# A soft mixture of experts on one core: the output product made transposed in float32 on four row groups

## The chip, the core and the metric

One core of a Trainium2 chip runs one program. The time is device microseconds for the whole program, here the median of three runs. The engines that matter are TensorE (PE, with its weight loads shown as PEld), VectorE (DVE), ScalarE (ACT), GpSimd (POOL) and SyncE (SP), whose queue issues every transfer.

## The reference

The input x is 8 sequences of 2496 tokens with 256 values each. The reference takes the real part of a two-dimensional Fourier transform of each sequence and feeds the 19968 tokens to a soft mixture of experts with 8 experts of 4 slots, 32 slots in all:

```python
X = np.fft.fft(np.fft.fft(x, axis=1), axis=2).real        # 8 x 2496 x 256, then 19968 x 256
logits = X @ phi                                            # 19968 x 32
d = softmax(logits, over the tokens);  slot_input = d.T @ X # 32 x 256
slot_out[e] = relu(slot_input[e] @ w1[e]) @ w2[e]           # 32 x 256
c = softmax(logits, over the 32 slots)                      # 19968 x 32
out = c @ slot_out                                          # 19968 x 256, float32
```

The change concerns the last line alone: 19968 tokens by 32 slots, times 32 slots by 256 values, 20.45 MB of float32.

## The kernel before, in words

The sequences are taken in four pairs, p = 0 to 3. The length 2496 is split as 64 times 39, and mirrored columns are folded, so that the 2496 tokens of a sequence become 64 values of an index a by 20 columns k in two mirror halves. Parts a, t, b and c (line 210 on) load x, fold it and make the logits; parts e, d and u turn the token weights back and gather the slot inputs; part m joins the four pairs; parts l (line 465) and v (line 484) are the two expert products. All of this is the first 136 us, and the change does not touch it. What follows is touched.

Part r (line 498) takes the expert sums out of PSUM (`sos`, lines 506 and 507), replicates the 32 slots to four groups of 32 partitions with one product (line 508), and splits the result into a rounded part `rh[0]` (lines 510 and 511, ACT) and a remainder `rh[1]` (line 513, DVE). Both are 128 by 512, block diagonal for two columns k, and zero elsewhere (a memset, line 502).

Part s (line 520), once for each pair, transposes the logits so that the 128 partitions are tokens (lines 527 and 532), and makes the softmax over slots: in two halves of 20 columns k, a maximum (541, DVE), a subtraction (542, POOL), an exponential (543, ACT), a sum and reciprocal (544 to 546, DVE) and a product (547, POOL). The result `c` has 128 tokens on the partitions and 20 times 32 values behind each.

Part q (line 549) splits each half of `c` into a rounded part (553, ACT) and a remainder (554, DVE), side by side, in the single-pass type float32r.

Part o (line 560) runs 20 times, five for each pair. It transposes four blocks of 128 by 128 on TensorE (567), copies them out of PSUM (568, ACT), and makes four products of 128 tokens by two columns k by 256 values (574), each as two accumulating matmuls, with `rh[0]` and with `rh[1]`. The token weights `lT` are the stationary operand, the expert sums move. Each product fills one PSUM bank of 512 values and is copied to an output tile `ot` by ACT and DVE in turn (578). A finished tile of 8 KB on each partition (1 MB) leaves through SP (585). The fifth tile of each pair leaves in two pieces, 768 KB and, for the column that is its own mirror, 128 KB from 64 partitions (583). The first tile of all leaves in three pieces.

The output tiles are a ring of six (`RING`). The products use the pools `bank` (2 banks) and `bank3` (3 banks), the transposes `bank1` (2 banks). `ORDER` (line 39) lists the parts in priority; a planner with a cost model of its own then sets the order on each engine's queue, and an engine runs its queue in that order.

Of the kernel before, what the change touches and what calls it, by code (L numbers as in the profile page):

```python
# [6 lines left out]
F32 = mybir.dt.float32  # L7
F32R = mybir.dt.float32r
AF = mybir.ActivationFunctionType
ALU = mybir.AluOpType  # L10
# [4 lines left out]
NA, NCF, NKC = 64, 39, 20  # L15
NPAIR = 4
D = 256
NSLOT = 32
# [17 lines left out]
FIRST = [0, 1]  # L36
P1, P2, P3, PM = 2, 2, 3, 0
W2 = [1, 1, 1, 1, 1, 1, 1, 1, 1, 1, 1, 2, 2, 1]
ORDER = (
# [6 lines left out]
).split()  # L46

# [66 lines left out]
    return out, where  # L114


def _build(nc, tc, xh, phih, w1h, w2h, cins, where, out, out0):
    from contextlib import ExitStack, nullcontext

    v, sc, pe = nc.vector, nc.scalar, nc.tensor  # L120
    ctx = ExitStack()
    with ctx:
        cp = ctx.enter_context(tc.tile_pool(name="cp", bufs=1))
        sb = ctx.enter_context(tc.tile_pool(name="sb", bufs=1))
# [4 lines left out]
        def ring(name):  # L129
            return sb.tile([128, 8, D], F32, name=name, tag="ring", bufs=RING)  # L130
# [19 lines left out]
        def bank1(name, dt=F32):  # L150
            return p1.tile([128, 512], dt, name=name, tag="p1")
# [33 lines left out]
        ps = bank("psphi")  # L185
# [14 lines left out]
        tok = cp.tile([128, NPAIR], F32, name="tok")  # L200
# [219 lines left out]
        anchor = {}  # L420
# [41 lines left out]
        rh = []  # L462
# [34 lines left out]

        def part_r():
            so = sos_[0]
            for j in range(2):  # L500
                rh.append(sb.tile([128, 2, D], F32R, name=f"rh{j}", tag="d", bufs=2))
                nc.gpsimd.memset(rh[j].bitcast(F32), 0.0)
            v.tensor_copy(identr, ident)
            sos = sb.tile([128, D], F32, name="sos", tag="dpm", bufs=2)
            ps = bank("sorep")
            sc.copy(sos[:, :128], so[:, :128])
            v.tensor_copy(sos[:, 128:], so[:, 128:D])
            pe.matmul(ps[:, :D], C("sel2"), sos, start=True, stop=True)
            half = [slice(0, 64), slice(64, 128)]
            sc.copy(rh[0][half[0], 0, :], ps[half[0], :D])  # L510
            (v.tensor_copy if RH else sc.copy)(rh[0][half[1], 1, :], ps[half[1], :D])
            for k, r in enumerate(half):
                v.tensor_tensor(rh[1][r, k, :], ps[r, :D], rh[0][r, k, :].bitcast(F32), op=ALU.subtract)

        identr = sb.tile([128, 128], F32R, name="identr", tag="mex2", bufs=1)


        hl, cq = {}, {}

        def part_s(p):  # L520
            L = lt[p]
            cq[p] = sb.tile([128, 40, NSLOT], F32, name=f"c{p}", tag=CT[p], bufs=bufs_(CT[p]))
            for b in range(3):
                ps = bank1(f"cT{p}_{b}")
                n = min(4, NG - 4 * b)
                for j in range(n):
                    pe.transpose(  # L527
                        ps[:, 120 * j : 120 * j + 120],
                        L[:, 4 * b + j].rearrange("p s k -> p (s k)"), ident[:120, :120],
                    )  # L530
# [5 lines left out]
            e1 = nc.gpsimd if GP & 1 else v  # L536
            e2 = nc.gpsimd if GP & 2 else v
            for i in range(2):
                c = cq[p][:, 20 * i : 20 * i + 20]
                m = sb.tile([128, 2, 20], F32, name=f"cm{p}_{i}", tag="cm", bufs=2)  # L540
                v.tensor_reduce(m[:, 0], c, axis=AX.X, op=ALU.max)  # L541
                e1.tensor_tensor(c, c, m[:, 0].unsqueeze(2).to_broadcast([128, 20, NSLOT]), op=ALU.subtract)  # L542
                sc.activation(c, c, AF.Exp)
# [3 lines left out]
                e2.tensor_tensor(c, c, m[:, 1].unsqueeze(2).to_broadcast([128, 20, NSLOT]), op=ALU.mult)  # L547

        def part_q(p, i):
            c = cq[p][:, 20 * i : 20 * i + 20]  # L550
            e3 = nc.gpsimd if GP & 4 else v
            t = sb.tile([128, 20, 2, NSLOT], F32R, name=f"hl{p}_{i}", tag=HT[i], bufs=bufs_(HT[i]))
            sc.copy(t[:, :, 0], c)
            e3.tensor_tensor(t[:, :, 1], c, t[:, :, 0].bitcast(F32), op=ALU.subtract)
            hl[p, i] = t


        n_ev = [0]

        def part_o(p, b):  # L560
            ps = bank1(f"lT{p}_{b}", F32R)
            lT = et([128, 4, 128], f"lTs{p}_{b}", F32R)
            with tc.issue_after(anchor["v1"]) if LA and p == 0 else nullcontext():
              for i in range(4):
                k0 = 8 * b + 2 * i
                src = hl[p, k0 // 20][:, k0 % 20 : k0 % 20 + 2].rearrange("p k h s -> p (k h s)")
                pe.transpose(ps[:, i * 128 : i * 128 + 128], src, identr)  # L567
            sc.copy(lT, ps.rearrange("p (i n) -> p i n", i=4))  # L568
            ot = ring(f"o{p}_{b}")
            done = 0  # L570
            for i in range(4):
                po = (bank, bank3)[i % 2](f"po{p}_{b}_{i}")
                for j in range(2):
                    pe.matmul(  # L574
                        po, lT[:, i, :], rh[j].rearrange("p k d -> p (k d)"), start=j == 0, stop=j == 1,
                    )
                np_ = 64 if b == 4 and i == 3 else 128
                (v.tensor_copy if n_ev[0] % 2 else sc.copy)(  # L578
                    ot[:np_, 2 * i : 2 * i + 2, :].rearrange("p k d -> p (k d)"), po[:np_]
                )  # L580
                n_ev[0] += 1
                if b == 4 and i == 3:
                    nc.sync.dma_start(out0[p].rearrange("p (r d) -> p r d", d=D), ot[:64, 6:8])
                elif i == 3 or (b == 4 and i == 2) or ((p, b) == (0, 0) and i in FIRST):
                    nc.sync.dma_start(
                        out[p, :, (8 * b + done) * D : (8 * b + 2 * i + 2) * D].rearrange("p (r d) -> p r d", d=D),
                        ot[:, done : 2 * i + 2],
                    )
                    done = 2 * i + 2

        def after(f, *a):
            at_ = {0: None, 1: anchor.get("u"), 2: anchor.get("l")}[CAFTER]
# [63 lines left out]
```

## Time and profile before

| | |
|---|---|
| median of three runs (lowest, highest) | 197.49 us (197.16, 197.59) |
| span of the profiled execution, first to last instruction | 195.7 us |
| launch and end around the span, taken as 197.49 less 195.7 | 1.8 us |
| PE, PEld, DVE, ACT, POOL busy, share of the span | 88%, 63%, 67%, 65%, 13% |
| HBM read, written | 38.46 MB, 20.45 MB |
| mean granted TensorE clock | 0.988 of full speed |

The page gives no time of its own for the profiled execution beside its span; where a sum is made against the span, the 1.8 us are added back. In the rows below a time in the first column is counted from the start of the span. `L574` is line 574 of the kernel before. A row of a group gives count, busy time in us, mean length of one in ns, and after the bar the idle time before them with what ended it. Matmuls on TensorE overlap, so that a mean length is longer than the distance between two of them. A float32 matmul shows as two records.

### The profile page before, as it was taken

To read this page: it belongs to the slowest core of one execution; us is meant where nothing else is said; L and a number is where in the kernel's file an instruction comes from. 1 tells how busy PE (TensorE), PEld (TensorE's weight loads), DVE (VectorE), ACT (ScalarE), POOL (GpSimd) and SP (SyncE) were. 2 spreads that over 40 slices of the span, in tenths; PEclk is the share of its full clock that TensorE was granted. 3 is DMA by queue.
4 is the path that set the end of the run, shared out by engine and by line. 5 is a ranking of instruction groups with operands and counts; after the bars stand their busy time and mean duration, and the time that the engine had idled before them with its cause. 6 is when DMAs were issued, how large, how long until landed. Compare 5 with 4: busy or idle time off the path is not lost.

```text
span 195.7 us, 4290 instructions
## 1 busy us (share of the span) xinstructions
PE 173.1 (88%) x1690; PEld 124.3 (63%) x1690; DVE 131.5 (67%) x238; ACT 127.4 (65%) x277; POOL 24.6 (13%) x27
## 2 busy tenths in 40 slices
PE   0499999979999999989999989999999999989900
PEld 0376685557768877567765857256788867768600
DVE  0599868999977973712457534895777888966600
ACT  2135675579767696676848756754877988997610
POOL 0000000000000000000000202577003257310000
PEclk9999999999999999999999999999999999999995
DMA  5999999999970899200770969970199999799996
GB/s 182 406 424 411 422 415 422 419 422 373 372 286 8 266 383 425 104 0 0 240 284 20 321 230 343 417 308 0 64 384 375 407 403 398 304 417 365 430 427 214
DMA packets 10707, 59.17 MB, mean 302 GB/s; under 512 B 1344, under 2 KB 1728, under 8 KB 5696
## 3 DMA queue, kind: packets, MB, share of 16 engines
q1 hardware_dynamic: 10688, 58.91, 76.7%
q8 instruction: 13, 0.21, 0.4%
q14 instruction: 6, 0.05, 0.1%
HBM read 38.46 MB, written 20.45 MB: 301 GB/s over the span
## 4 chain that ended last, share of the span: by engine, by line
PE 79%; ACT 8%; DVE 3%; DMA 2%; POOL 2%; issue 2%; SPq 0%; ACTq 0%; DVEq 0%; POOLq 0%
PE po L574 17%; PE pt L231 10%; PE z L238 8%; PE e L329 7%; PE a L273 6%; PE u L371 6%; PE d L346 4%; PE h L470 4%; PE so L490 4%; PE lp L291 3%; PE lm L292 3%; PE cT L527 3%; DMA x<-xh 2%; PE lT L567 2%; POOL c L542 2%; ACT et L232 2%
## 5 line engine op out<-in xcount | busy, mean ns | idle before, releaser
L574 PE MATMUL po<-rh,lTs 128*128 128x512 f32 x160 | 42.4, 405 | 1.6 <-ACT lTs L568 0.7
L231 PE MATMUL pt<-cs,eo 128*128 128x128 f32 x160 | 26.4, 297 | 8.7 <-DVE eo L226 7.6
L574 PEld LDWEIGHTS po<-rh,lTs 128*128 128x128 f32 x160 | 28.1, 188 | 8.6 <-ACT o L578 1.8
L578 DVE COPY o<-po 128x512 f32<-128x512 f32 (+1 forms) x40 | 26.9, 685 | 7.9 <-PE po L574 6.9
L232 ACT COPY et<-pt 128x512 f32<-128x512 f32 x40 | 23.0, 594 | 13.8 <-PE pt L231 13.2
L231 PEld LDWEIGHTS pt<-cs,eo 128*128 128x128 f32 x160 | 19.5, 151 | 15.5 <-DVE eo L226 7.6
L578 ACT COPY o<-po 128x512 f32<-128x512 f32 x40 | 23.2, 595 | 7.4 <-PE po L574 7.1
L224 DVE TENSOR_TENSOR x<-x 128x1024 f32<-128x1024 f32 x16 | 19.4, 1214 | 3.2 <-DMA x<-xh 3.2
L238 PE MATMUL z<-et,wphi 128*32 128x256 f32 (+1 forms) x288 | 19.0, 371 | 0.9 <-ACT et L232 0.8
L542 POOL TENSOR_TENSOR c<-c,cm 128x640 f32<-128x640 f32 x8 | 11.8, 1487 | 28.0 <-DVE cm L541 27.0
L314 ACT ACTIVATE d<-lt,nm 120x128 f32<-120x128 f32 x44 | 13.6, 392 | 2.1 <-DVE nm L311 2.0
L226 DVE TENSOR_TENSOR eo<-x 128x512 f32<-128x512 f32 x20 | 13.6, 681 | 0.6 <-PE u L371 0.3
L227 DVE TENSOR_TENSOR eo<-x 128x512 f32<-128x512 f32 x20 | 13.6, 678 | 0.0
L329 PE MATMUL e<-cs,dpm 120*64 120x120 f32 x176 | 13.5, 273 | 0.0
L238 PEld LDWEIGHTS z<-et,wphi 128*32 128x32 f32 x288 | 7.8, 113 | 8.3 <-ACT et L232 3.2
L329 PEld LDWEIGHTS e<-cs,dpm 120*64 120x64 f32 x176 | 10.7, 136 | 3.5 <-issue 2.0
L354 ACT COPY ds<-d 64x320 f32<-64x320 f32 x24 | 10.0, 420 | 4.1 <-PE d L346 3.4
L547 POOL TENSOR_TENSOR c<-c,cm 128x640 f32<-128x640 f32 x8 | 11.0, 1389 | 10.0 <-DVE cm L546 5.5
L568 ACT CAST lTs<-lT 128x512 fp32r<-128x512 f32 x20 | 11.5, 600 | 0.9 <-PE lT L567 0.9
L273 PE MATMUL a<-cs,zt 128*120 128x128 f32 x88 | 11.4, 279 | 0.6 <-ACT zt L264 0.6
L371 PE MATMUL u<-eo,ds 128*32 128x129 f32 x320 | 11.6, 275 | 0.0
L273 PEld LDWEIGHTS a<-cs,zt 128*120 128x120 f32 x88 | 10.2, 183 | 1.9 <-ACT zt L264 1.3
(99 smaller groups left out, 245.3 us busy)
## 6 DMA issues: line engine op xcount, KB each, us to landing
x<-xh SPq DMA_DIRECT2D x16, 1024.0 KB, 11.2
out<-o SPq DMA_DIRECT2D x15, 1024.0 KB, 5.8
w<-w1h SPq DMA_DIRECT2D x6, 1024.0 KB, 9.2
w<-w2h SPq DMA_DIRECT2D x12, 512.0 KB, 6.0
x<-xh SPq DMA_DIRECT2D x4, 896.0 KB, 11.0
out<-o SPq DMA_DIRECT2D x4, 768.0 KB, 6.1
w<-w1h SPq DMA_DIRECT2D x4, 512.0 KB, 6.3
w<-w2h SPq DMA_DIRECT2D x2, 1024.0 KB, 6.9
```

The source lines that it names most:

```text
L224: v.tensor_tensor(x[:, 0:4], x[:, 0:4], x[:, 4:8], op=ALU.add)
L226: v.tensor_tensor(e[:, :, 0:128], x[:, 0:4, 0:128], x[:, 0:4, 128:256], op=ALU.add)
L227: v.tensor_tensor(e[:, :, 128:256], x[:, 0:4, 0:128], x[:, 0:4, 128:256], op=ALU.subtract)
L231: pe.transpose(b[:, g * 128 : g * 128 + 128], e[:, g, k * 128 : k * 128 + 128], ident)
L232: sc.copy(tr[k][:, :, :, qi, :], b.rearrange("p (g h a) -> p g h a", g=4, h=2))
L238: pe.matmul(z[32 * g : 32 * g + 32, o : o + n], wphi[:, w, :], tr[k][:, g].rearrange("p h q a -> p (h q a)"), start=i != 1, stop=i != 0, t ...
L273: pe.matmul(ps[:120, i * 128 : i * 128 + 128], zt[p][:, GS * g : GS * g + GS].rearrange("p s h c -> p (s h c)"), C("wa"), start=True, stop ...
L329: pe.matmul(ps[64 * k : 64 * k + 64, 120 * i : 120 * i + 120], dpm[p, hf][:, k, 3 * j + i, :], C(name), start=True, stop=True, tile_positi ...
L371: last = pe.matmul(ub[32 * g : 32 * g + 32, 0:129], dsb[p][:, k, c, :], e[:, 0:129] if k == 0 else e[:, 127:256], start=cc == 0, stop=cc == 9,
L542: e1.tensor_tensor(c, c, m[:, 0].unsqueeze(2).to_broadcast([128, 20, NSLOT]), op=ALU.subtract)
L574: pe.matmul(po, lT[:, i, :], rh[j].rearrange("p k d -> p (k d)"), start=j == 0, stop=j == 1,)
L578: (v.tensor_copy if n_ev[0] % 2 else sc.copy)(ot[:np_, 2 * i : 2 * i + 2, :].rearrange("p k d -> p (k d)"), po[:np_])
```

## The change

The output product is turned round. The expert sums become the stationary operand and stay float32 (`rh[0]`, one tile of 128 by 256, four copies of the 32 slots), the token weights move, and the result has 128 of the 256 values on the partitions and tokens behind them. For this the 32 slots must lie on partitions: VectorE's block transpose turns each 32 by 32 block of `c`, so that partition group g holds the slots of the 32 tokens that were on it. The four groups are multiplied one by one, each with 32 rows of the array (`tile_position=(32 * g, 0)`), into four PSUM banks. The split into rounded part and remainder, TensorE's transposes and their copies, the zeroed block-diagonal tiles and the small 128 KB transfers go. The columns k are now cut 16 and 24 in place of 20 and 20 (`KP`); the tiles b = 0 to 3 take 16 columns and one half of the 256 values, the tile b = 4 the last eight columns and both halves. The products go round seven banks, those of `bank1` among them. In `ORDER`, `q01` and `q11` come earlier and `s20` moves ahead of `o10`. The host undoes the new layout.

```diff
+KP = ((0, 16), (16, 24))
-    "u30 m00 l00 s00 l10 q00 s10 v00 v10 r00 o00 q01 o01 q10 o02 o03 "
-    "o04 o10 s20 q11 o11 q20 o12 o13 q21 o14 s30 o20 o21 q30 o22 o23 "
+    "u30 m00 l00 s00 l10 q00 s10 v00 q01 v10 r00 o00 o01 q10 o02 q11 o03 "
+    "o04 s20 o10 o11 q20 o12 o13 q21 o14 s30 o20 o21 q30 o22 o23 "
...
         def part_r():
             so = sos_[0]
-            for j in range(2):
-                rh.append(sb.tile([128, 2, D], F32R, name=f"rh{j}", tag="d", bufs=2))
-                nc.gpsimd.memset(rh[j].bitcast(F32), 0.0)
-            v.tensor_copy(identr, ident)
+            rh.append(sb.tile([128, D], F32, name="rh", tag="mex2", bufs=1))
...
-            pe.matmul(ps[:, :D], C("sel2"), sos, start=True, stop=True)
-            half = [slice(0, 64), slice(64, 128)]
-            sc.copy(rh[0][half[0], 0, :], ps[half[0], :D])
-            (v.tensor_copy if RH else sc.copy)(rh[0][half[1], 1, :], ps[half[1], :D])
-            for k, r in enumerate(half):
-                v.tensor_tensor(rh[1][r, k, :], ps[r, :D], rh[0][r, k, :].bitcast(F32), op=ALU.subtract)
+            for k in range(2):
+                dk = slice(128 * k, 128 * k + 128)
+                pe.matmul(ps[:, dk], C("sel2"), sos[:, dk], start=True, stop=True)
+            v.tensor_copy(rh[0], ps[:, :D])
...
         def part_q(p, i):
-            sc.copy(t[:, :, 0], c)
-            e3.tensor_tensor(t[:, :, 1], c, t[:, :, 0].bitcast(F32), op=ALU.subtract)
+            r0, n = KP[i]
+            t = sb.tile([128, n, NSLOT], F32, name=f"ct{p}_{i}", tag=HT[i], bufs=bufs_(HT[i]))
+            v.transpose(t.rearrange("p k s -> p (k s)"), cq[p][:, r0 : r0 + n].rearrange("p k s -> p (k s)"))
...
+        BANKS = [bank, bank3, bank1, bank3, bank, bank1, bank3]
         def part_o(p, b):
-            ps = bank1(f"lT{p}_{b}", F32R)
-            lT = et([128, 4, 128], f"lTs{p}_{b}", F32R)
-                pe.transpose(ps[:, i * 128 : i * 128 + 128], src, identr)
-            sc.copy(lT, ps.rearrange("p (i n) -> p i n", i=4))
-            for i in range(4):
-                po = (bank, bank3)[i % 2](f"po{p}_{b}_{i}")
-                for j in range(2):
-                    pe.matmul(
-                        po, lT[:, i, :], rh[j].rearrange("p k d -> p (k d)"), start=j == 0, stop=j == 1,
-                    )
+            if b < 4:
+                t, r0, dcs = hl[p, b // 2], 0, [b % 2]
+            else:
+                t, r0, dcs = hl[p, 1], 16, [0, 1]
+            for g in range(4):
+                n = 16 if b < 4 else 8 if g < 2 else 6
+                w = n * NSLOT
+                po = BANKS[n_ev[0] % 7](f"po{p}_{b}_{g}")
+                rows = slice(32 * g, 32 * g + 32)
+                mv = t[rows, r0 : r0 + n].rearrange("p k s -> p (k s)")
+                for j, dc in enumerate(dcs):
+                    pe.matmul(
+                        po[:, j * w : j * w + w], rh[0][rows, 128 * dc : 128 * dc + 128], mv,
+                        start=True, stop=True, tile_position=(32 * g, 0),
+                    )
+                (v.tensor_copy if n_ev[0] % 2 else sc.copy)(ot[:, o : o + w * len(dcs)], po[:, : w * len(dcs)])
...
-                if b == 4 and i == 3:
-                    nc.sync.dma_start(out0[p].rearrange("p (r d) -> p r d", d=D), ot[:64, 6:8])
...
+                if g == 3 or (p, b) == (0, 0):
+                    nc.sync.dma_start(out[p, b, :, done:o], ot[:, done:o])
```

More of the change, by code (lines that the diff above doesn't have):

```diff
@@ L35 @@
 GP = 3
-FIRST = [0, 1]
 P1, P2, P3, PM = 2, 2, 3, 0
@@ L114, in _tables, with _build @@
     return out, where
-def _build(nc, tc, xh, phih, w1h, w2h, cins, where, out, out0):
+def _build(nc, tc, xh, phih, w1h, w2h, cins, where, out):
     from contextlib import ExitStack, nullcontext
@@ L507, in part_r @@
             v.tensor_copy(sos[:, 128:], so[:, 128:D])
-            pe.matmul(ps[:, :D], C("sel2"), sos, start=True, stop=True)
-            half = [slice(0, 64), slice(64, 128)]
-            sc.copy(rh[0][half[0], 0, :], ps[half[0], :D])
-            (v.tensor_copy if RH else sc.copy)(rh[0][half[1], 1, :], ps[half[1], :D])
-            for k, r in enumerate(half):
-                v.tensor_tensor(rh[1][r, k, :], ps[r, :D], rh[0][r, k, :].bitcast(F32), op=ALU.subtract)
-        identr = sb.tile([128, 128], F32R, name="identr", tag="mex2", bufs=1)
+            for k in range(2):
+                dk = slice(128 * k, 128 * k + 128)
+                pe.matmul(ps[:, dk], C("sel2"), sos[:, dk], start=True, stop=True)
+            v.tensor_copy(rh[0], ps[:, :D])
         hl, cq = {}, {}
@@ L535, in part_s @@
                 )
[L536 to L540, printed above, removed]
+            for i, (r0, n) in enumerate(KP):
+                c = cq[p][:, r0 : r0 + n]
+                m = sb.tile([128, 2, 24], F32, name=f"cm{p}_{i}", tag="cm", bufs=2)[:, :, :n]
                 v.tensor_reduce(m[:, 0], c, axis=AX.X, op=ALU.max)
-                e1.tensor_tensor(c, c, m[:, 0].unsqueeze(2).to_broadcast([128, 20, NSLOT]), op=ALU.subtract)
+                nc.gpsimd.tensor_tensor(c, c, m[:, 0].unsqueeze(2).to_broadcast([128, n, NSLOT]), op=ALU.subtract)
                 sc.activation(c, c, AF.Exp)
@@ L546, in part_s @@
                 v.reciprocal(m[:, 1], m[:, 1])
-                e2.tensor_tensor(c, c, m[:, 1].unsqueeze(2).to_broadcast([128, 20, NSLOT]), op=ALU.mult)
+                nc.gpsimd.tensor_tensor(c, c, m[:, 1].unsqueeze(2).to_broadcast([128, n, NSLOT]), op=ALU.mult)
         def part_q(p, i):
-            c = cq[p][:, 20 * i : 20 * i + 20]
-            e3 = nc.gpsimd if GP & 4 else v
-            t = sb.tile([128, 20, 2, NSLOT], F32R, name=f"hl{p}_{i}", tag=HT[i], bufs=bufs_(HT[i]))
-            sc.copy(t[:, :, 0], c)
@@ L562, in part_o @@
-            lT = et([128, 4, 128], f"lTs{p}_{b}", F32R)
-            with tc.issue_after(anchor["v1"]) if LA and p == 0 else nullcontext():
-              for i in range(4):
[L565 to L570, printed above, removed]
@@ L571, in part_o @@
-            for i in range(4):
-                po = (bank, bank3)[i % 2](f"po{p}_{b}_{i}")
-                for j in range(2):
+            ot = ring(f"o{p}_{b}").rearrange("p r d -> p (r d)")
+            if b < 4:
+                t, r0, dcs = hl[p, b // 2], 0, [b % 2]
+            else:
+                t, r0, dcs = hl[p, 1], 16, [0, 1]
+            done = o = 0
+            for g in range(4):
[5 more added lines that the diff above has]
+                for j, dc in enumerate(dcs):
@@ L574, in part_o @@
                     pe.matmul(
-                        po, lT[:, i, :], rh[j].rearrange("p k d -> p (k d)"), start=j == 0, stop=j == 1,
-                    )
-                np_ = 64 if b == 4 and i == 3 else 128
-                (v.tensor_copy if n_ev[0] % 2 else sc.copy)(
-                    ot[:np_, 2 * i : 2 * i + 2, :].rearrange("p k d -> p (k d)"), po[:np_]
-                )
+                        po[:, j * w : j * w + w], rh[0][rows, 128 * dc : 128 * dc + 128], mv,
+                        start=True, stop=True, tile_position=(32 * g, 0),
+                    )
@@ L581, in part_o @@
+                (v.tensor_copy if n_ev[0] % 2 else sc.copy)(ot[:, o : o + w * len(dcs)], po[:, : w * len(dcs)])
+                o += w * len(dcs)
                 n_ev[0] += 1
-                if b == 4 and i == 3:
[L583 to L589, printed above, removed]
+                if g == 3 or (p, b) == (0, 0):
+                    nc.sync.dma_start(out[p, b, :, done:o], ot[:, done:o])
+                    done = o
@@ L637 @@
     ]
-    out = nc.dram_tensor("out", (NPAIR, 128, 38 * D), F32, kind="ExternalOutput").ap()
-    out0 = nc.dram_tensor("out0", (NPAIR, 64, 2 * D), F32, kind="ExternalOutput").ap()
+    out = nc.dram_tensor("out", (NPAIR, 5, 128, 8 * D), F32, kind="ExternalOutput").ap()
     with tile.TileContext(nc, schedule_with_timeline_sim=True) as tc:
-        _build(nc, tc, *ins[:4], ins[4:], where, out, out0)
+        _build(nc, tc, *ins[:4], ins[4:], where, out)
     r = _run(nc, [arrays], core_ids=[0])
-    got = r.results[0]["out"].reshape(NPAIR, 2, NA, 19, 2, D)
-    got0 = r.results[0]["out0"].reshape(NPAIR, NA, 2, D)
+    got = r.results[0]["out"]
+    main = got[:, :4].reshape(NPAIR, 2, 2, 128, 2, 2, 8, 2, 32)
+    tok = np.empty((NPAIR, 2, 2, NKC, NA, D), np.float32)
+    tok[:, :, :, :16] = main.transpose(0, 7, 4, 1, 6, 5, 8, 2, 3).reshape(NPAIR, 2, 2, 16, NA, D)
+    o = 0
+    for g in range(4):
+        n = 4 if g < 2 else 3
+        last = got[:, 4, :, o : o + 2 * n * 64].reshape(NPAIR, 128, 2, n, 2, 32)
+        o += 2 * n * 64
+        tok[:, :, g // 2, 16 : 16 + n, 32 * (g % 2) : 32 * (g % 2) + 32] = last.transpose(0, 4, 3, 5, 2, 1).reshape(
+            NPAIR, 2, n, 32, D
+        )
     full = np.empty((NPAIR, 2, 2496, D), np.float32)
@@ L648 @@
     kc, ka = k % NCF, k % NA
-    for h in range(2):
-        for half, sel in ((0, (kc > 0) & (kc < NKC)), (1, kc >= NKC)):
-            row = kc[sel] - 1 if half == 0 else NCF - kc[sel] - 1
-            full[:, h, k[sel]] = got[:, half, ka[sel], row, h]
-        sel = kc == 0
-        full[:, h, k[sel]] = got0[:, ka[sel], h]
+    row = np.where(kc == 0, NKC - 1, np.where(kc < NKC, kc, NCF - kc) - 1)
+    full[:, :, k] = tok[:, :, (kc >= NKC).astype(int), row, ka]
     return full.reshape(8 * 2496, D)
```

## The prediction

> **What bounds the kernel now.** I read the page first, then the busy time by stretches, then the chain that ended last and the timelines of the engines around the first output.
>
> ```profile
> span 195.7 us, 4290 instructions
> ```
>
> ```profile
> 138.00:186.30 48.30, 46.71 (x246) 36.67 (x246) 37.83 (x63) 39.03 (x73) 11.15 (x8) 1.00 0.90 362
> 141.00:194.00 53.00, 43.89 (x233) 34.35 (x232) 35.02 (x59) 36.99 (x69) 11.15 (x8) 0.97 0.96 386
> 141.00:149.00 8.00, 8.00 (x45) 6.68 (x45) 5.57 (x9) 5.87 (x12) 0.00 (x0) 1.00 0.97 389
> 150.00:162.00 12.00, 11.59 (x69) 9.12 (x68) 10.36 (x20) 10.79 (x22) 4.99 (x4) 1.00 1.00 415
> 180.00:191.00 11.00, 6.12 (x28) 4.30 (x26) 4.25 (x7) 4.58 (x8) 0.00 (x0) 1.00 1.02 423
> 149.00:150.00 1.00, 1.00 (x6) 0.82 (x5) 0.70 (x1) 0.72 (x2) 0.00 (x0) 1.00 0.64 160
> 162.00:163.00 1.00, 1.00 (x8) 0.60 (x7) 1.00 (x3) 1.00 (x3) 0.70 (x1) 1.00 0.82 270
> 167.00:169.00 2.00, 1.88 (x11) 1.46 (x11) 2.00 (x6) 1.82 (x5) 0.00 (x0) 1.00 0.39 153
> 178.00:180.00 2.00, 2.00 (x13) 1.68 (x11) 1.28 (x3) 1.45 (x4) 0.00 (x0) 1.00 0.99 301
> 191.00:192.00 1.00, 0.00 (x0) 0.00 (x0) 0.00 (x0) 0.00 (x0) 0.00 (x0) 0.52 0.90 207
> ```
>
> These are stretches of the span: length, busy time of PE, PEld, DVE, ACT and POOL, then granted clock, busy share of the DMA engines and GB/s. The first row looks like a stage bound by TensorE: 46.71 of 48.30 us busy. But from 180 to 191 TensorE is busy for 6.12 us only: it ends near 186, while bytes move until 194 (386 GB/s for 53.0 us are the whole 20.45 MB). Almost 8 us of transfers are still to come when the last product is done. From 141 to 194 the DMA engines are 96% busy, and 20.45 MB leave at 386 GB/s. In undisturbed stretches the rate is 415 and 423, so 419 is the ceiling that I use, and 20.45 MB at 419 take 48.8 us. The stage is bound by the transfers, with 53.0 - 48.8 = 4.2 us of losses, which lie in a few places. A faster TensorE cannot by itself give more than those losses and an earlier first transfer.
>
> Two kinds of loss can be named. The first:
>
> ```profile
> L583 SPq DMA_DIRECT2D out<-o x4: 472/609/1220, 148.2 to 186.0; - x4
> ...
> DMA to landing us min/median/max: 3.1/4.9/6.9
> ```
>
> These are the four small transfers of 128 KB from 64 partitions. One is issued for each pair, 148.2 to 186.0, and lands some us later; after each there is one dip in GB/s with the engines still nearly busy. Against 419 the rows at 149, 162, 178 and 191 lose 0.62 + 0.36 + 0.56 + 0.51 = 2.05 us. The second is 167 to 169, with the DMA engines 39% busy: 2 x (1 - 153/419) = 1.27 us lost because nothing was queued. The chain of waits shows why:
>
> ```profile
> 161.42 0.75 DVE cm L541
> 162.30 3.68 POOL c L542 x2
> 166.01 0.20 ACT c L543
> ```
>
> The copies out of PSUM stand on the ACT and DVE queues behind the next pair's softmax, which waits for POOL. With TensorE needing about as long for a tile as the transfer of it, no stock of finished tiles covers that.
>
> **The change part by part.** The costs of the old output product:
>
> ```profile
> L574 PE MATMUL po<-rh,lTs 128*128 128x512 f32 x160 | 42.4, 405 | 1.6 <-ACT lTs L568 0.7 <-ACT o L578 0.6 <-ACT rh L511 0.2
> ...
> L574 PEld LDWEIGHTS po<-rh,lTs 128*128 128x128 f32 x160 | 28.1, 188 | 8.6 <-ACT o L578 1.8 <-ACT lTs L568 1.8 <-issue 0.3
> L578 DVE COPY o<-po 128x512 f32<-128x512 f32 (+1 forms) x40 | 26.9, 685 | 7.9 <-PE po L574 6.9
> ...
> L578 ACT COPY o<-po 128x512 f32<-128x512 f32 x40 | 23.2, 595 | 7.4 <-PE po L574 7.1
> ...
> L568 ACT CAST lTs<-lT 128x512 fp32r<-128x512 f32 x20 | 11.5, 600 | 0.9 <-PE lT L567 0.9
> ...
> L567 PE MATMUL lT<-identr,hl 128*128 128x128 f32 x80 | 9.0, 243 | 0.0
> ...
> L554 DVE TENSOR_TENSOR hl<-c,hl 128x640 fp32r<-128x640 f32 x8 | 7.1, 883 | 0.0
> ...
> L527 PE MATMUL cT<-cs,lt 120*128 120x120 f32 x44 | 6.1, 271 | 0.0
> ...
> L482 DVE STREAM_TRANSPOSE hT<-hs 128x512 f32<-128x512 f32 x4 | 2.7, 678 | 0.1
> ```
>
> *TensorE.* A tile of 1 MB now costs 42.4/20 = 2.12 us of products and 9.0/20 = 0.45 us of transposes, which overlap a little, against 1.049/0.419 = 2.50 us for its transfer. After the change a tile costs four float32 matmuls of 512 columns on 32 rows each. No row here shows row groups. The nearest is the first expert product, also float32, 512 columns and cut in four, but by output columns:
>
> ```profile
> L470 PE MATMUL h<-w,sT x64: 592/592/617, 121.7 to 129.6; 128*32 128x512 f32 x64
> ```
>
> ```profile
> 121.66 2.78 PE L470 MATMUL h<-w,sT 128*32 128x512 f32 x24
> ```
>
> The code has 32 such matmuls and the trace 64 records, so each is two records. 24 records took 2.78 us; with the last one's tail of about 0.17 (0.592 less the distance) taken off, a set of four records takes (2.78 - 0.17)/6 = 0.43 us. That four really run at once is seen from an undivided float32 product:
>
> ```profile
> 111.75 2.55 PE L346 MATMUL d<-e,cs 128*128 128x320 f32 x8
> ```
>
> There eight records of 320 columns take 2.55 us, about 0.3 us each with the tail, or 0.4 to 0.5 for 512 columns: one undivided record costs what the set of four does. So the new tile costs 2 x 0.43 = 0.86 us if the four row groups run at once, 1.72 if two do, and 8 x 0.43 = 3.44 if they take turns. Eight weight loads of 128 columns at 188 ns, if nothing hid them and they came singly, are 1.5 us. I take 0.9 to 1.7 us; anything below 2.50 gives the same end, since the transfers then set the pace. The Trainium skill (page "TensorE: Matmul & The Clock Gate", section "Part 3: Packing small matmuls") gives four row groups of 512 columns a measured speedup of 3.07; by that a tile would cost an estimated 3.44/3.07 = 1.1 us. No run here shows it yet, and the sum would be the same.
>
> *ACT and DVE.* The copies stay 80, taken in turn, four for a tile: 2 x 0.685 = 1.37 us of DVE and 2 x 0.595 = 1.19 us of ACT, each under 2.50. ACT loses the 20 casts of `lT` (11.5 us) and the rounding in part q. DVE loses the remainders (7.1 us) and gains block transposes: 512 elements cost 0.678, 768 in proportion 1.02, so 4 x 1.70 = 6.8 us. DVE is even, ACT lighter by over 11.5 us. POOL and the reductions handle the same number of elements, cut 16 and 24. All of it is beside the transfers and costs nothing while tiles are in stock; tiles will be in stock, since two engines empty a tile in 1.4 us where its transfer takes 2.5, and the ring holds six. That stock also covers a queue that waits for POOL: the 1.27 us go. What is late next is the ring itself: copies will wait for a transfer to free a tile, and behind them on ACT and DVE stands the next pair's softmax, with up to five tiles, 12 us, to cover it.
>
> *Transfers.* The bytes are the same: 4 x (4 x 128 x 2048 + 128 x 1792) x 4 = 20.45 MB. The four 64-partition transfers go, their bytes travel in full-width tiles of 7 KB rows: 2.05 us saved. The first tile leaves in four pieces rather than three. Of the slow start (141 to 149 at 389 GB/s, 8 x (1 - 389/419) = 0.57 us) I count half, 0.3, as saved.
>
> *First output.*
>
> ```profile
> 136.53 0.70 PE L508 MATMUL sorep<-sos,cs 128*128 128x256 f32 x2
> ...
> 137.29 0.38 ACT L510 CAST rh<-sorep 64x256 fp32r<-64x256 f32 x1
> ...
> 138.07 0.86 DVE L513 TENSOR_TENSOR rh<-sorep,rh 64x256 fp32r<-64x256 f32 x2 [1.60 <-ACT rh L511]
> ...
> 139.63 1.28 ACT L578 COPY o<-po 128x512 f32<-128x512 f32 x2 [0.22 <-PE po L574]
> ...
> 140.24 0.35 SPq L585 DMA_DIRECT2D out<-o  x1
> ```
>
> Now: two ACT casts, then two subtractions until 138.93, then products; the first copy starts at 139.63. After: the replicating product, in two halves with the same columns, ends about as before; one DVE copy of 256 elements, priced like one of the two subtractions at 0.43, from 137.29 to 137.72; then the first matmul, two records, 0.43 + 0.59 = 1.02 us with up to 0.19 of weight load; the copy starts at 138.8 to 139.0. The first transfer is 0.7 us earlier. Bounds: 1.2 earlier if the first half's early start counts, 1.0 later if the two transposes of the next part q (0.68 + 1.02) stand ahead of the copy on DVE.
>
> *Sum.* 2.05 + 1.27 + 0.3 + 0.7 = 4.3 us. 195.7 - 4.3 = 191.4 us of span, plus the 1.8 us around it (197.49 - 195.7): 193.2 us.
>
> **The rivals.**
>
> *The row groups take turns.* Against it: the column groups above run at once. For it: nothing in this trace shows rows divided. For each pair TensorE then needs 4 x 3.44 + 8 x 0.43 x 1792/2048 = 16.8 us, for four 67.1, plus half of the 6.1 us of softmax transposes (L527, two pairs of four): from 137.7 to 207.9, then a copy, 0.7, the last tile's transfer, 2.5, and the 1.7 from 194.0 to the end: span 212.8, time 215 us. It decides as soon as a tile costs over 2.50 us, that is with fewer than 1.4 groups at once. Chance 0.11.
>
> *The clock falls.* With TensorE idle since about 186 the row at 191 shows a clock of 0.52. If the lighter TensorE lost its clock during the stage, two groups at once would cost 2 x 1.72 = 3.44 us for a tile, again 215 us, but four at once 1.72 and no harm. Against it: pauses would be about 1.5 us, not 5. The Trainium skill (same page, "Part 1: The HAM clock gate") has the clock halve after an idle window of about 3.4 us; the row at 191 agrees. Chance 0.02.
>
> *Only the small transfers matter.* The queues stall as before and the first output is no earlier: 197.5 - 2.05 - 0.3 = 195.1 us. For it: the softmax chain over ACT, DVE and POOL is kept, and the planner orders it anew. Against it: the stock of tiles. Chance 0.10.
>
> *Nothing remains.* A planner's order that puts several softmax steps ahead of the first output delays it by about 4 us and eats the gain: 197.5, or a little over. Chance 0.05.
>
> **How the numbers follow.** My forecast has chance 0.72. Its own range is 191.6 (start 1.2 earlier, all 4.2 us of losses gone, 423 GB/s in place of 419) to 194.9 (start 1.0 later). The range for all is 191.5 to 196.8, reaching over the third rival with a start 1.7 late; it leaves out the first two, and most of the fourth. Faster by over 0.2% (0.4 us, about what a measurement of this kernel can tell from no change): 0.72 + 0.10 = 0.82; within that 0.03; slower 0.11 + 0.02 + 0.02 = 0.15.
>
> **What would show it.** Right: the records of a tile's four matmuls start together and a tile takes 0.9 to 1.7 us; the first output transfer is issued near 139.5; GB/s stays near 419 from there, with no dips in the stage; TensorE idles at the ring. Wrong: matmul records of different groups one behind another and TensorE busy to the end; clock below 1.00 in the stage; gaps in DMA share behind a softmax; the first issue after 140.24.

## The result and the profile after

The changed kernel takes 203.05 us (median of four runs, 202.1 to 203.3), beside 197.32 us for the kernel before on the same chip: ratio 1.0287 [1.026, 1.0314]. It is 5.7 us slower. The forecast was 193.2 us with a range up to 196.8 us; the result lies outside it, on the other side of no change. Medians and ratios here and below leave out the slow runs: two of the four of e2_filler (212.56 and 217.09 us, with a mean clock of 0.954 and 0.928), one of e8_no_small_transfers (902.92 us) and one of the kernel before beside e5 to e8 (414.61 us).

The page of the changed kernel: span, two rows of the slices, and the groups that carry the output (L562 is the product, L566 the copy out of PSUM).

```profile
span 201.5 us, 4131 instructions
...
PEclk9999999999999999999999999999996555557955
DMA  5999999999941998003925879911994995849994
...
L562 PE MATMUL po<-ct,rh 32*128 32x512 f32 (+2 forms) x192 | 43.8, 700 | 2.9 <-DVE o L566 2.4
...
L566 ACT COPY o<-po 128x512 f32<-128x512 f32 (+1 forms) x40 | 21.3, 580 | 15.8 <-PE po L562 15.7
L566 DVE COPY o<-po 128x512 f32<-128x512 f32 (+1 forms) x40 | 24.6, 662 | 7.2 <-PE po L562 7.2
```

The copies cost about what they did (0.580 and 0.662 us for 0.595 and 0.685). The transposes of the token weights, their copies and the second product are gone. What is new are the low digits near the end of the DMA row: the transfers stop three times. The stretches of the output stage give the sizes (columns as in the prediction's first table: PE, PEld, DVE, ACT, POOL, granted clock, DMA share, GB/s).

```profile
140.00:152.00 12.00, 11.81 (x79) 6.88 (x76) 9.55 (x17) 8.57 (x17) 1.82 (x2) 1.00 0.99 399
152.00:156.00 4.00, 2.40 (x10) 1.53 (x9) 3.43 (x8) 3.03 (x6) 1.71 (x2) 0.62 0.21 86
156.00:168.00 12.00, 12.00 (x36) 6.81 (x35) 4.83 (x9) 2.71 (x5) 1.48 (x1) 0.50 1.02 420
168.00:176.00 8.00, 8.00 (x28) 5.26 (x28) 6.43 (x13) 4.86 (x9) 4.38 (x4) 0.50 0.60 249
176.00:182.00 6.00, 5.40 (x21) 3.44 (x20) 3.52 (x6) 2.00 (x5) 0.62 (x1) 0.50 0.58 232
```

Against 419 GB/s the rows lose 0.57, 3.18, 0.00, 3.25 and 2.68 us: 9.7 us, where the kernel before lost 4.2. The table also shows what the forecast had given a chance of 0.02: from 153 to 183 us the granted clock is 0.50.

The start went as predicted. The timeline ahead of the first transfer:

```profile
137.22 0.42 DVE L508 COPY rh<-sorep 128x256 f32<-128x256 f32 x1 [0.58 <-PE sorep L507]
...
137.70 2.98 PE L562 MATMUL po<-ct,rh 32*128 32x512 f32 x17 [0.52 <-DVE rh L508]
...
138.86 1.56 ACT L566 COPY o<-po 128x512 f32<-128x512 f32 x3 [2.54 <-PE po L562]
...
139.47 0.82 SPq L570 DMA_DIRECT2D out<-o  x2
```

The first copy starts at 138.86 and the first transfer is issued at 139.47, 0.77 us earlier than before. The row groups work at once: four records of the four groups start within 0.02 us of each other, the next four 0.53 us later, and the next tile's first 0.43 us after those, so that the first tile of eight records takes 0.96 us.

The chain of waits through the first gap:

```profile
149.51 0.60 DVE cm L531
150.11 0.07 issue
150.18 2.49 POOL c L532 x2
152.67 0.02 issue
152.69 0.85 ACT c L533
153.54 0.02 issue
153.57 0.95 DVE cm L534
154.52 0.61 DVE o L566
155.13 0.04 issue
155.17 1.21 PE po L562
```

This is the softmax of the third pair (maximum on DVE, subtraction on POOL, exponential on ACT, sum on DVE), and at its end a copy of an output piece, for which TensorE waits. The timeline of DVE shows the copy behind the softmax:

```profile
149.42 1.53 DVE L531 TENSOR_REDUCE cm<-c 128x16 f32<-128x512 f32 x2
150.87 0.68 DVE L566 COPY o<-po 128x512 f32<-128x512 f32 x1
151.92 0.69 DVE L534 TENSOR_REDUCE cm<-c 128x16 f32<-128x512 f32 x1 [0.36 <-ACT c L533]
...
153.57 0.95 DVE L534 TENSOR_REDUCE cm<-c 128x24 f32<-128x768 f32 x1 [0.47 <-ACT c L533]
154.44 0.68 DVE L566 COPY o<-po 128x512 f32<-128x512 f32 x1
```

Which copy that is, SP's transfers tell. They leave in the written order, as their sizes show: the first tile in four pieces, the other four of the first pair in one each, so that the ninth is the first tile of the second pair. SP's issues on both sides of the gap:

```profile
139.47 7.30 SPq L570 DMA_DIRECT2D out<-o  x8
155.18 0.81 SPq L570 DMA_DIRECT2D out<-o  x2
```

Its waits for VectorE from 139 to 165 us (us in total, times, the longest):

```profile
SPq L570 <- DVE o L566: 15.4, 7, 8.4
```

Eight transfers are issued until 146.77 us and the ninth at 155.18, after a wait of 8.4 us for a copy of VectorE; the copy that starts at 154.44 ends at 155.12. The tenth, the next tile, follows at once: it was ready before. Behind the first pair's copies VectorE makes six up to there, two for each tile. So the last piece of the first tile of the second pair stands behind four copies for later tiles and behind the softmax of the third pair, and no tile leaves before this one. From 153 to 156 us almost nothing moves. No TensorE work is in the chain of this gap from 148.83 us, a copy on DVE, to 155.13, and the clock was 1.00 until 152.9: the half clock did not make the first gap. The gaps at 168 and at 176 fall in the softmax of the last pair; ahead of them the chain is TensorE's own work at half clock, from 159.63 to 169.28 us.

### The profile page after: what moved, and what is told of

Same layout as the page of the kernel before. It is cut to its first block, busy times and chain, and to the rows that moved or that the text cites. A ratio compares the mean times of both kernels' runs of the same rounds, so it can differ in the third digit from the quotient of the medians.

```text
span 201.5 us, 4131 instructions
## 1 busy us (share of the span) xinstructions
PE 172.6 (86%) x1644; PEld 114.0 (57%) x1644; DVE 129.0 (64%) x236; ACT 110.7 (55%) x247; POOL 20.8 (10%) x25
## 4 chain that ended last, share of the span: by engine, by line
PE 73%; ACT 7%; DVE 6%; issue 3%; DMA 2%; POOL 1%; POOLq 1%; DVEq 0%; SPq 0%; ACTq 0%
PE po L562 15%; PE pt L231 9%; PE z L238 8%; PE e L329 6%; PE a L273 5%; PE u L371 5%; PE d L346 4%; PE h L470 4%; PE so L490 3%; PE cT L519 3%; PE lp L291 3%; PE lm L292 3%; DMA x<-xh 2%; DVE o L566 2%; ACT et L232 2%
## 5 line engine op out<-in xcount | busy, mean ns | idle before, releaser
L562 PE MATMUL po<-ct,rh 32*128 32x512 f32 (+2 forms) x192 | 43.8, 700 | 2.9 <-DVE o L566 2.4
L562 PEld LDWEIGHTS po<-ct,rh 32*128 32x128 f32 x192 | 25.6, 239 | 17.7 <-DVE o L566 7.5
L566 ACT COPY o<-po 128x512 f32<-128x512 f32 (+1 forms) x40 | 21.3, 580 | 15.8 <-PE po L562 15.7
L566 DVE COPY o<-po 128x512 f32<-128x512 f32 (+1 forms) x40 | 24.6, 662 | 7.2 <-PE po L562 7.2
L532 POOL TENSOR_TENSOR c<-c,cm 128x512 f32<-128x512 f32 (+1 forms) x8 | 10.0, 1264 | 75.3 <-DVE cm L531 72.2
L524 ACT COPY c<-cT 128x480 f32<-128x480 f32 (+1 forms) x12 | 6.0, 516 | 10.3 <-PE cT L519 10.3
L537 POOL TENSOR_TENSOR c<-c,cm 128x512 f32<-128x512 f32 (+1 forms) x8 | 10.1, 1263 | 8.4 <-DVE cm L536 8.4
```

The lines of the kernel that those rows point to most:

```text
L562: pe.matmul(po[:, j * w : j * w + w], rh[0][rows, 128 * dc : 128 * dc + 128], mv, start=True, stop=True, tile_position=(32 * g, 0),)
L566: (v.tensor_copy if n_ev[0] % 2 else sc.copy)(ot[:, o : o + w * len(dcs)], po[:, : w * len(dcs)])
```

## The experiments

The experiments ran on several chips; each ratio is to the kernel before on the same chip (medians of 197.5 to 197.7 us). My theory after the trace (*queue theory*): the change leaves the transfers as the bound and gives enough room, but the order of the queues uses it up, in two ways, softmax steps ahead of copies and tiles finished out of turn. Its rival (*clock theory*): the half clock makes TensorE late, and the gaps follow from that.

### The softmax left out: e1_no_softmax

```diff
-    "o04 s20 o10 o11 q20 o12 o13 q21 o14 s30 o20 o21 q30 o22 o23 "
-    "q31 o24 o30 o31 o32 o33 o34"
+    "o04 o10 o11 o12 o13 o14 o20 o21 o22 o23 "
+    "o24 o30 o31 o32 o33 o34"
...
-                t, r0, dcs = hl[p, b // 2], 0, [b % 2]
+                t, r0, dcs = hl[p % 2, b // 2], 0, [b % 2]
...
```

> The changed kernel, but the softmax of the third and fourth pair is left out of the output stage and their tiles use the token weights of the first and second pair. Queue theory (the planner's order puts the next pair's softmax ahead of copies, tiles finish out of turn, TensorE starves and the clock falls as a consequence): no gap in the transfers, 419 GB/s from 140.3 to about 189, clock 1.00 or nearly, time 192 to 194 us. Clock theory (the product on row groups leaves so much of the array idle that the clock is halved whatever the queues do, and then a tile costs over 2.5 us): the clock falls to 0.50 in the stage all the same, time 198 to 204 us.

Measured: 194.0 us, ratio 0.9804 [0.9774, 0.9834]. Its stretches:

```profile
152.00:168.00 16.00, 15.19 (x65) 8.06 (x63) 8.39 (x14) 7.17 (x14) 0.00 (x0) 0.61 1.02 420
168.00:176.00 8.00, 7.20 (x35) 4.67 (x33) 4.22 (x7) 3.35 (x7) 0.00 (x0) 0.71 1.01 416
```

No gap, and the clock falls all the same (0.61, 0.71): the time is that of the queue theory, the clock that of its rival. The half clock alone makes no gap. This run also takes work from every engine; the same work in another order is e3_in_order.

### A filler for TensorE: e2_filler

One more matmul of 128 rows and 512 columns for each tile, into a bank that nobody reads.

```diff
...
+            with tc.issue_after(ins.ins):
+                pe.matmul(
+                    fill_[0], rh[0][:, :128], t[:, 0:16].rearrange("p k s -> p (k s)"), start=True, stop=True,
+                )
```

> The changed kernel with one more matmul behind each output tile, 128 rows by 128 columns by 512, float32, into a PSUM bank that nobody reads: only to keep TensorE at work. Queue theory: the clock stays near 1.00, but the first gap of the transfers, near 152 to 156, stays (3.2 us) and later ones stay in part; time 198 to 203 us. Clock theory: with the clock back at 1.00 a tile with its filler costs 1.9 us, under 2.5, and the time is 193 to 196 us.

Measured: 206.4 us (206.43 and 206.46), ratio 1.0439 [1.04, 1.0478], mean clock 0.988. The clock is back and the time is longer, above what either theory expected. The clock theory as stated, that a full clock brings 193 to 196 us, falls; but the filler adds time of its own, and what remains of the theory is taken up below.

### Both disciplines at once: e3_in_order

From part r on, each instruction of PE, ACT and DVE is tied behind the one before it in the written order, without a semaphore; the softmax of the last two pairs is cut in four steps (x the transposes, y maximum and subtraction, z exponential, w sum and quotient), a tile apart, so that POOL works while the copies of a tile go on. In `ORDER`, `q10` and `q11` also move ahead of the first tile.

```diff
...
-    "o04 s20 o10 o11 q20 o12 o13 q21 o14 s30 o20 o21 q30 o22 o23 "
...
+    "x20 o10 y20 o11 z20 o12 w20 o13 q20 q21 o14 x30 o20 y30 o21 z30 o22 w30 "
...
+            for i in list(nc.cur_bb.bb.instructions)[n0:]:
+                if i.engine in kept:
+                    if i.engine in last:
+                        tc.add_manual_dep(
...
+                    last[i.engine] = i.name
```

> The changed kernel with the same work; from the replicated expert sums on, PE, ACT and DVE run their output-stage instructions in written order, tile by tile, and the softmax of pairs three and four is written in four steps, each a tile apart. Queue theory: no gap, 193 to 194.5 us. Clock theory: the clock falls all the same; if the four row groups then stay together a tile costs 1.7 us and the time is 193 to 195 us, if not about 3.2 us and the time 200 us or more.

Measured: 193.65 us, ratio 0.9794 [0.9762, 0.9826]. Its stretches:

```profile
140.00:152.00 12.00, 10.60 (x75) 6.56 (x71) 9.88 (x18) 8.82 (x17) 2.48 (x2) 1.00 1.00 402
152.00:156.00 4.00, 3.27 (x19) 2.81 (x18) 3.86 (x10) 3.12 (x7) 2.22 (x2) 0.59 1.01 417
156.00:168.00 12.00, 10.17 (x44) 5.37 (x45) 8.48 (x16) 5.97 (x11) 2.79 (x3) 0.71 1.01 418
168.00:176.00 8.00, 6.21 (x39) 4.11 (x40) 7.17 (x13) 3.81 (x9) 2.52 (x2) 0.61 1.01 418
```

The same work, a low clock here too (0.59 to 0.71), no gap: 0.6 us of losses, nearly all in the first row. So a change of order alone removes the whole loss of the changed kernel, and more.

### The former order line: e4_old_order

```diff
-    "u30 m00 l00 s00 l10 q00 s10 v00 q01 v10 r00 o00 o01 q10 o02 q11 o03 "
+    "u30 m00 l00 s00 l10 q00 s10 v00 v10 r00 o00 q01 o01 q10 o02 o03 "
...
```

> The changed kernel with the ORDER line of the kernel before (one part of the change undone). Both theories: the planner's queues in the second half of the stage are the same, so 202 to 204 us; if the new ORDER is the cause of the loss, 193 to 198 us.

Measured: 204.74 us, ratio 1.0364 [1.0318, 1.0409]. The new priorities in `ORDER` are not what made the kernel slower; without them it is no better.

### The old product with the same discipline: e5_before_in_order

The kernel before, with the ties and the four softmax steps of e3_in_order, and the transposes of a tile issued one tile ahead (part `L`).

```diff
-    "u30 m00 l00 s00 l10 q00 s10 v00 v10 r00 o00 q01 o01 q10 o02 o03 "
+    "u30 m00 l00 s00 l10 q00 s10 v00 q01 v10 q10 L00 L01 r00 q11 o00 L02 o01 L03 o02 L04 o03 L10 o04 "
...
```

> The kernel before, its old product and its small transfers kept, with the discipline of e3: written order on PE, ACT and DVE from the expert sums on, the transposes of a tile one tile ahead of its products, the softmax of pairs three and four in four steps a tile apart. If the new product is what makes room (a tile costs TensorE 2.2 to 2.5 us here, so no stock of tiles): 196 to 198 us. If the order alone is worth the 4 us of e3: 193 to 194 us.

Measured: 203.93 us, ratio 1.0364 [1.0301, 1.0427]. Both expectations were missed: this order is worth nothing to the old product, it even costs 3.6%. TensorE's products are 61% of its chain from 140 us on, their transposes 10%. My reading, not tried by itself, is that with about as long for a tile as its transfer takes, a rigid order makes TensorE late at each wait, so that the room that e3_in_order uses comes from the change. Other orders for the old product were not tried.

### One half of the discipline: e6_pieces_in_turn

Only the parts o are tied to one another; the softmax is one piece again and free for the planner.

```diff
...
+            if what[0] != "o":
+                continue
...
```

> The changed kernel with its own ORDER; only the matmuls and copies of the output tiles are held to written order on each engine, and the planner still puts the softmax steps where it likes between them. If the tiles finished out of turn are the loss: 193.5 to 196 us. If the softmax steps ahead of copies are the loss: 199 to 203 us.

Measured: 200.27 us, ratio 1.0144 [1.0112, 1.0177]. The first gap is gone (416 GB/s from 152 to 156 us). Two of its stretches, where a gap stays, with the softmax of the last pair in the chain (POOL's subtraction at 163.35 us):

```profile
164.00:168.00 4.00, 2.97 (x12) 0.88 (x6) 2.90 (x8) 2.99 (x6) 2.89 (x3) 1.00 0.49 203
168.00:172.00 4.00, 2.07 (x5) 0.30 (x4) 2.89 (x5) 1.24 (x3) 1.48 (x1) 0.74 0.46 193
```

From 164 to 168 us the clock is 1.00, but from 156 to 164 it was 0.56 on average, so this run alone does not tell order and clock apart.

### The other half: e9_softmax_held

The kernel and `ORDER` of e3_in_order, but only the four softmax steps and part q are tied, behind the copies that stand ahead of them; products and copies are free. The edit, against e3_in_order:

```diff
-                    if i.engine in last:
+                    if i.engine in last and what[0] in "xyzwq":
...
-                    last[i.engine] = i.name
+                    if what[0] == "o":
+                        last[i.engine] = i.name
```

> The changed kernel with the softmax of the last two pairs cut in four steps, each held on the queues of TensorE, ScalarE and VectorE behind the copies that stand ahead of it in ORDER, as in e3_in_order; the products and copies of the output tiles are free for the planner, which still puts the fourth piece of some tiles behind copies of later tiles. It is the other half of e6_pieces_in_turn. If the place of the softmax steps is the larger part of the loss and the disorder of the tiles costs only while ScalarE or VectorE waits, the time is 194 to 197 us and the gaps in GB/s at 153 and at 168 are gone or short. If tiles finished out of turn are the larger part, the time is 199 to 203 us and a gap of some us remains after each first tile of a pair whose fourth copy is late.

Measured: 200.3 us, ratio 1.0146 [1.009, 1.0202]. The first gap is gone, but from 164 to 171 us the transfers run at 77 GB/s:

```profile
164.00:171.00 7.00, 7.00 (x18) 3.33 (x19) 2.74 (x4) 2.88 (x6) 2.49 (x2) 0.50 0.19 77
```

The timelines of DVE, PE and SP there (L519 the softmax's transposes, L542 its maximum, L579 the product, L583 the copy, L587 the transfer):

```profile
167.45 1.55 DVE L542 TENSOR_REDUCE cm<-c 128x16 f32<-128x512 f32 x2 [5.45 <-ACT c L524]
168.92 1.28 DVE L583 COPY o<-po 128x512 f32<-128x512 f32 x2
```

```profile
162.29 1.86 PE L519 MATMUL cT<-cs,lt 120*128 120x120 f32 x8
164.08 2.08 PE L579 MATMUL po<-ct,rh 32*128 32x512 f32 x6
166.10 0.86 PE L519 MATMUL cT<-cs,lt 120*128 120x120 f32 x3
166.89 4.82 PE L579 MATMUL po<-ct,rh 32*128 32x512 f32 x8
```

```profile
160.83 9.11 SPq L587 DMA_DIRECT2D out<-o  x2
```

Here the planner put products between the softmax's transposes. The maximum waits for the last three transposes, and behind it on DVE, idle for 5.45 us, stand copies whose products were done at 166.16. The two issues of SP in its line are that of 160.83 and the next, which is through at 169.94; between them it issues nothing. So the two kinds of disorder feed each other: products out of turn delay the softmax, and the softmax delays copies. TensorE is busy in all of these 7 us at a clock of 0.50, and its work is the chain there; what a full clock would save of this gap was not tried. Either discipline alone brings the ratio from 1.029 to 1.014 or 1.015, a half of the way back to the kernel before; both bring it to 0.979 (0.984 in a second set). Each alone gives 1.4 points, both 4.5 to 4.9: the first gap goes with either, the one in the last pair only with both.

### What the half clock costs: e7_in_order_filler

e3_in_order with the filler of e2_filler.

> e3 with the filler matmul of e2 behind each tile. The clock should stay nearer to 1.00 than the 0.93 of e3. If the clock costs nothing where the tiles come in turn, the time is that of e3, 193 to 194.5 us; if the half clock still costs something in e3, 191.5 to 193 us; if the filler itself is what cost time in e2, 197 us or more.

Measured: 196.1 us, ratio 0.9932 [0.9903, 0.9962]. The clock is 1.00 through the stage, and by the ratios the kernel is slower than e3_in_order by 2 to 3 us (0.9932 for 0.9794, and for 0.9841 in the second set). None of the three expectations named this time. A tile takes 1.07 us here, with its filler 2.13, and there are gaps again (358 GB/s in 152 to 156, 311 in 164 to 168). About 2.13 is what a tile would cost at half clock without the filler. So the run cannot price the clock, but e3_in_order bounds it: with 0.6 us of losses in all, most of them at a clock of 1.00, a full clock has almost nothing to give there.

### What the clock follows: e11_filler_32_rows

e7_in_order_filler with the filler on 32 rows.

```diff
-            pe.matmul(fill_[0], rh[0][:, :128], t[:, 0:16].rearrange("p k s -> p (k s)"), start=True, stop=True)
+            pe.matmul(
+                fill_[0], rh[0][:32, :128], t[:32, 0:16].rearrange("p k s -> p (k s)"), start=True, stop=True,
+                tile_position=(0, 0),
+            )
```

> e7_in_order_filler with the filler matmul of each tile (float32, 512 columns) on the first 32 rows of the array only, so that it adds the same time and a quarter of the rows. Only the granted clock is asked for. If the clock follows how long TensorE has no matmul at all, it stays near 1.00 through the stage as with the filler on 128 rows. If it follows how much of the array works, it falls to 0.5 within the stage as in e3_in_order (mean 0.93). Time 194 to 197 us in both cases.

Measured, in a single run: 198.32 us, mean clock 0.915. The late part of the stage, first with the filler on 128 rows, then on 32:

```profile
176.00:188.00 12.00, 9.94 (x54) 3.16 (x50) 7.18 (x12) 5.26 (x10) 0.00 (x0) 1.00 1.01 416
```

```profile
176.00:188.00 12.00, 12.00 (x34) 5.84 (x33) 4.80 (x8) 4.15 (x8) 0.00 (x0) 0.50 0.80 331
```

With 32 rows TensorE has matmuls in all of the 12 us and still runs at 0.50. Busy time is not what the clock follows here; rows at work are the difference between the two kernels, and with them the filler's overlap with products of other groups (a tile with its filler takes 1.72 us at full clock, against 2.13). The expected time was missed: at half clock a tile with its filler takes 3.41 us (the fillers start at 176.54, 179.96 and 183.37 us), over the 2.50 of its transfer, and the transfers starve (331 GB/s).

### The small transfers: e8_no_small_transfers

The kernel before, with the 128 KB transfer issued for the first pair alone.

```diff
-                    nc.sync.dma_start(out0[p].rearrange("p (r d) -> p r d", d=D), ot[:64, 6:8])
+                    if p == 0:
+                        nc.sync.dma_start(out0[p].rearrange("p (r d) -> p r d", d=D), ot[:64, 6:8])
```

> The kernel before with the 128 KB transfer of the last three pairs left out, so that these output rows are not written. If each costs what its dip shows (0.51 us beyond its own 0.31 us of bytes) the time falls by 2.5 us, to about 195.2; if the dips cost nothing, by 0.9 us at most, to 196.7; if TensorE sets the end of the stage, no change.

Measured: 195.94 us, ratio 0.9923 [0.9898, 0.9949], that is 1.5 us [1.0, 2.0] for three. Of this 3 x 0.131 MB at 419 GB/s, 0.94 us, is their own bytes, which the change does not save. Some 0.2 us is left for each (0.0 to 0.35 by the interval), 0.8 for four. Two of the rows with a dip (270 and 301 GB/s in the kernel before), now without these transfers:

```profile
162.00:163.00 1.00, 1.00 (x10) 0.73 (x8) 1.00 (x2) 1.00 (x4) 0.49 (x1) 1.00 0.50 205
178.00:180.00 2.00, 2.00 (x12) 1.63 (x11) 1.26 (x3) 1.65 (x3) 0.00 (x0) 1.00 0.96 392
```

The dip at 178 is gone. The one at 162 stays without the small transfer, and there the DMA engines are half idle.

### The first half earlier: e10_in_order_again and e12_halves

e12_halves is e3_in_order with the expert sums copied in two halves out of two banks, each as soon as it is there; e10_in_order_again is e3_in_order beside it.

```diff
...
-                pe.matmul(ps[:, dk], C("sel2"), sos[:, dk], start=True, stop=True)
-            v.tensor_copy(rh[0], ps[:, :D])
+                ps = (bank, bank3)[k](f"sorep{k}")
+                pe.matmul(ps[:, :128], C("sel2"), sos[:, dk], start=True, stop=True)
+                v.tensor_copy(rh[0][:, dk], ps[:, :128])
```

> The kernel of e3_in_order again, beside e12_halves on one chip, for an interval: 193.65 us give or take 0.4, ratio to before 0.98, by every theory.

> e3_in_order with the expert sums copied in two halves out of two PSUM banks, the first as soon as its half of the replicating product is there. If the start of the first output sets the rest of the time, the first output is issued 0.3 to 0.5 us earlier and the time is 193.1 to 193.4 us. If the first tile waits for the second half in any case, or the transfers take up the gain, the time is that of e10_in_order_again.

Measured: 194.3 us (194.09 to 194.6), ratio 0.9841 [0.9816, 0.9867], and 193.66 us (193.16 to 193.86), ratio 0.9805 [0.9778, 0.9832]. The first issue, of e10_in_order_again and of e12_halves:

```profile
139.35 1.33 SPq L587 DMA_DIRECT2D out<-o  x3
```

```profile
138.86 1.81 SPq L587 DMA_DIRECT2D out<-o  x4
```

It comes 0.49 us earlier and the time falls by 0.64 us; the two sets of runs do not overlap. Both medians lie some 0.3 us above what was expected, their order is as expected. Once the transfers run without gaps, an earlier start goes through to the end. e12_halves is faster than both kernels: 3.8 us under the kernel before on that chip (197.47), some 9 under the changed one.

## Why the prediction was wrong

*What bounds the kernel*: right. With the gaps gone, the stage runs at 417 to 418 GB/s from 152 us on, and its time is the transfers' plus the start and the end.

*TensorE*: right on the point that decided most, that the four row groups run at once. A tile takes 0.96 to 1.07 us at full clock, near the 0.86 of the row-by-row estimate and inside 0.9 to 1.7. The rival of groups that take turns is refuted. The Trainium skill's speedup of 3.07 gave an estimated 1.1 (page "TensorE: Matmul & The Clock Gate", section "Part 3: Packing small matmuls"); the traces give a little more, 3.44/1.07 = 3.2 in e7_in_order_filler and 3.44/0.96 = 3.6 in the changed kernel's first tile.

*First output*: right, 0.77 us for the predicted 0.7.

*Small transfers*: the direction was right, the term too large for the kernel before, about 0.8 us by e8_no_small_transfers for the predicted 2.05. The dips in GB/s after them were all put down to them, and the one at 162 us stays without its transfer. Also, probably, TensorE needed nearly as long for a tile as the transfer, so that filling a dip does not bring the last tile forward by as much. In e3_in_order all dips are gone together, so that the term cannot be read off there by itself.

*The step that failed* is the one on the stock: "tiles will be in stock, since two engines empty a tile in 1.4 us where its transfer takes 2.5, and the ring holds six. That stock also covers a queue that waits for POOL: the 1.27 us go." The sum of the engines' times was right, the conclusion from it was not. A stock is of finished tiles, and SP sends them in the written order. The planner, which goes by its own cost model, had at least three tiles in work at a time and put the last piece of the first behind the softmax. In place of 1.27 us that go there are gaps of 9.1 us, behind a softmax, which the prediction had named as a sign of being wrong. e3_in_order shows the working of the stock itself to be sound: with the queues kept in turn the kernel takes 193.65 us, by the mechanism of the forecast and close to its 193.2.

*The rivals*: "Nothing remains" named the planner, but put its disorder ahead of the first output and priced it at the gain, 197.5. The disorder came ahead of the sixth tile, and again in the softmax of the last pair, where nothing but stock could cover it. "Only the small transfers matter" did say that the planner would order the softmax anew, but met it with the stock of tiles, and priced it with the stalls of the kernel before; no row of that kernel could show the new order. A chance of 0.05 and a price of 4 us were both too small. "The clock falls" was right on the clock and wrong on the reason: it halved with no pause near 3.4 us, and, as that rival said for four groups at once, did no harm in the kernels without gaps, e1_no_softmax and e3_in_order.

*The sum*, worked out from the spans: the transfers, counted from 140 us in place of 141 (-1.0), and the losses, 9.7 for 4.2 us (+5.5), end at 140 + 48.8 + 9.7 = 198.5; from there to the end of the span it is 3.0 us in place of 1.7 (+1.3). In all that is the measured 201.5 - 195.7 = 5.8. For e10_in_order_again it is -1.0, 0.5 for 4.2 (-3.7), and 3.0 for 1.7 (+1.3), in all 192.3 - 195.7 = -3.4. The forecast had -0.7 for the start and -3.6 for the losses. The term at the end was not in it, since it kept the 1.7 us. Last stretches with bytes, of the kernel before and of e10_in_order_again:

```profile
193.00:194.00 1.00, 0.00 (x0) 0.00 (x0) 0.00 (x0) 0.00 (x0) 0.00 (x0) 0.50 0.92 387
194.00:195.00 1.00, 0.00 (x0) 0.00 (x0) 0.00 (x0) 0.00 (x0) 0.00 (x0) 0.50 0.05 18
```

```profile
189.00:190.00 1.00, 0.00 (x0) 0.00 (x0) 0.00 (x0) 0.00 (x0) 0.00 (x0) 0.50 0.33 136
190.00:191.00 1.00, 0.00 (x0) 0.00 (x0) 0.00 (x0) 0.00 (x0) 0.00 (x0) 0.50 0.07 29
```

Before, the DMA engines are busy almost to the end and then stop (0.92, 0.05); after the change their busy share trails off over two stretches (0.33, 0.07). Why the last tile ends so raggedly was not tried.

*What stays open*: how much of the 5.9 us of the later gaps of the changed kernel is due to the half clock; the first, 3.2 us, is not. Between 153 and 183 us its TensorE is busy for 27.8 of 30 us at 0.50, with pieces of one group that overlap with nothing, and there a full clock would probably help. The fillers cannot tell, since they add as much time as the clock gives back. That a full clock isn't needed, once the order is mended, is shown.

## What to carry to other kernels

When a change shortens the work of one engine, a planner writes the order of every queue anew, and the room gained can be lost there: price a disorder of the queues at what stands behind it, tile by tile, and look for pieces that the sending queue needs first. A buffer ring is a stock only if tiles are finished in the order in which they leave. After such a change, try what it brings to tie copies and products in turn and to cut long chains over several engines into steps a tile apart; here that made 203.05 into 193.65 us, and neither half of it alone did more than 3 us.

## What the runs showed of the hardware

- Four float32 matmuls on the four groups of 32 rows ran at once (starts within 0.02 us, 0.43 to 0.53 us for a set of 512 columns); two on the same group followed one another.
- The granted clock halved in a stage in which TensorE was nearly always busy. In the changed kernel it fell at 152.9 us, with no pause of TensorE above 0.5 us since 137.7; in e1_no_softmax at 152.2, with none above 0.8. The Trainium skill (page "TensorE: Matmul & The Clock Gate", section "Part 1: The HAM clock gate") ties the fall to an idle window of about 3.4 us; here the measurement decides against that as the only cause. In the ordered kernel a filler on 128 rows kept the clock at 1.00 (e7_in_order_filler, mean 0.98 to 0.99 in six runs); one on 32 rows with as many columns did not (e11_filler_32_rows, a single run). What exactly the clock follows, these runs do not show.
